# Sinkhorn-sorted attention and a bilinear FFN on one core: k and v of a head mixed together, v turned in two halves, units placed by a table

## The chip, the core and the metric

The kernel runs on one core of a Trainium2 chip. The core has TensorE (PE; its weight loads are shown as PEld), VectorE (DVE), ScalarE (ACT), GpSimd (POOL) and SyncE (SP), each with an instruction queue of its own that runs in order, and 16 engines for transfers (DMA). The metric is device time in microseconds (us) of one launch; less is better.

## What is computed

Cut to what matters (B, H, S, D = 4, 8, 768, 64; 8 blocks of 96 rows):

```python
P = sort_net                                   # 4, 8, 8, 8
for _ in range(5):
    P = np.exp(P - max(P, -1)); P = P / (sum(P, -1) + 1e-09)
    P = P / (sum(P, -2) + 1e-09)
k_sorted = einsum('bhij,bhjcd->bhicd', P, k_b)     # blocks of k mixed
v_sorted = einsum('bhij,bhjcd->bhicd', P, v_b)     # blocks of v mixed
attn = softmax(q_b @ k_sorted_b.T / sqrt(D))       # inside a block of 96
x = (attn @ v_sorted_b), heads side by side        # 3072 x 512
out = ((x @ w_a) * (x @ w_b)) @ w_out              # 512 -> 1536 -> 512
```

All inputs and the output are float32; the kernel works in bf16 with float32 sums in PSUM.

## The kernel before

Two heads form a pair `g`; four pairs make a batch, 16 pairs in all (`HP` = 4, `NPAIR` = 16). Row `6p + c` of a head lies on partition `p`, so each head's k, v and q arrive as a tile of 128 partitions by 6 chunks of 64 columns. `load_pair(g)` (line 93) issues the loads on GpSimd's queue, which convert float32 to bf16 on the way: k and v of both heads, and q for pairs from 4 on. Each tag has six buffers.

**Mixing.** `s_all` holds, for each head, P spread over the partitions. `pair_mix(g, "k")` (line 279) multiplies each chunk of k (64 weight columns) with `s_all` (128 moving columns): head 0 goes to PSUM partitions 0 to 63, head 1 to 64 to 127. That is 12 products for k and 12 for v. Four copies (ACT, ACT, then DVE, ACT) bring the results to `kT` and `vT`, of which there are three buffers (`NBUF`).

**Turning.** After this, k lies with its 64 columns on the partitions, as the scores need it. v has to be turned back: `turn_v(g)` (line 295) issues one transposing transfer of 128 x 1024 on SP's queue into `vs`. `pair_q(g)` (line 268) puts q of two heads side by side on GpSimd, and `turn_q(g)` (line 274) turns it on SP's queue.

**Scores and output.** `pair_scores(g)` (line 299) makes 2 x 8 score products and two exponentials on ACT (`eT`). `pair_o(g)` (line 314) calls `one_o` (line 244) twice: 8 products with a column of ones for the sum, reciprocal and scaling on DVE into `xp`. A transposing transfer on SP's queue then writes `xT`, which the FFN reads. `pair_o` also issues later loads, behind a `hold` (line 265): a copy of one element on GpSimd that waits until `xT` is there.

**The first batch** is done in two halves (blocks 0 to 3 and 4 to 7) by the functions named `half_` (lines 191 to 242); q is loaded for all of it at once (`q_first`), and q, v and x are turned by TensorE instead of by transfers.

**FFN.** `ffn_ab(b, m, t)` (line 349) makes 4 + 4 products of 384 columns (`pf`), a cast of `a` on ACT, and a product on DVE into `hT`. `ffn_out` (line 377) makes 12 products of 512 columns (`po`) in two steps, and a copy and a store.

**Order.** The order on the queues of all engines is the order in which the program issues instructions. `interleave(steps, units, spare, slow)` (line 451) runs the FFN steps of a batch and puts attention units of the next batch between them: M (mix), R (scores) and O (output), in the order of `units_full` (line 431), spread evenly by a formula. For batch 1 (24 steps) the units stand after steps 1, 2, 4, 5, 7, 8, 10, 11, 13, 14, 16, 17; for batches 2 and 3 (36 steps) after steps 1, 3, 5, 8, 10, 12, 15, 17, 19, 22, 24, 26. The order in both is M0, M1, R0, M2, R1, O0, M3, R2, O1, R3, O2, O3 (0 to 3 are the batch's pairs). M issues, in this order, k's mix, v's mix, `turn_v`, and for later pairs loads, `pair_q` and `turn_q` of the next pair.

Of the kernel before, what the change touches and what calls it, by code (L numbers as in the profile page):

```python
# [10 lines left out]
BF16 = mybir.dt.bfloat16  # L11
AF = mybir.ActivationFunctionType
# [10 lines left out]
def kernel(  # L23
# [43 lines left out]
    ld = ctx.enter_context(tc.tile_pool(name="ld", bufs=6))  # L67
# [18 lines left out]
    q_first = const.tile([P, H, W], BF16, name="q_first")  # L86
# [6 lines left out]
    def load_pair(g):  # L93
        base = 2 * g * S * D
        tiles = []
        for name, t in (("k2", k), ("v2", v), ("q2", q)):
            if g < HP and name == "q2":
                continue
            to = ld.tile([P, 2, W], BF16, tag=name, name=name)
            nc.gpsimd.dma_start(out=to, in_=_ap(t, base, [[W, P], [S * D, 2], [1, W]]))  # L100
            tiles.append(to)
        loaded[g] = tiles
# [5 lines left out]
    def load_ab(c):  # L108
        for w_ap, w_sb in ((moe_w_a, w_a_sb), (moe_w_b, w_b_sb)):
            nc.gpsimd.dma_start(  # L110
                out=w_sb[:, :, AB[c]:AB[c + 1]],
                in_=w_ap.rearrange("(kc p) n -> p kc n", p=P)[:, :, AB[c]:AB[c + 1]])
# [11 lines left out]
    for c in range(2):  # L124
        load_ab(c)
# [4 lines left out]
    kTs = [const.tile([P, S + PAD], BF16, name=f"kT{n}") for n in range(NBUF)]  # L130
    vTs = [const.tile([P, NB, P], BF16, name=f"vT{n}") for n in range(NBUF)]
    eTs = [const.tile([BLK, 2, 2, HB + PAD], BF16, name=f"eT{n}") for n in range(NBUF)]
    vss = [const.tile([P, NB, VW], BF16, name=f"vs{n}") for n in range(NBUF)]
    for t in kTs:
        nc.vector.memset(t[:, S:], 0.0)
        nc.vector.memset(t[:, HB:HB + PAD], 0.0)
    for t in vTs:
        nc.vector.memset(t[:, :, BLK:], 0.0)
# [6 lines left out]
    st = {}  # L145
# [29 lines left out]

    def first_q(hp):
        q_ps = psF.tile([P, NCH, P], BF16, tag="F", name="q_ps")
        for c in range(NCH):
            for e in range(2):
                nc.tensor.matmul(q_ps[e * D:(e + 1) * D, c, :],  # L180
                                 lhsT=q_first[:, 2 * hp + e, c * D:(c + 1) * D],
                                 rhs=ident, is_transpose=True)
        st["q_ps", hp] = q_ps

    def first_q_out(hp, eng):
        qT = const.tile([P, NB, NCH, CG], BF16, name=f"qT{hp}")
        copy(eng, qT.rearrange("p i c t -> p c i t"),
             st["q_ps", hp].rearrange("p c (i t) -> p c i t", i=NB))
        st["q", hp] = qT

    def half_mix(h, hp, what, eng, fill=0, cols=512):
        g = h * HP + hp
        src2 = loaded[hp][0 if what == "k" else 1]
        to = (kTs if what == "k" else vTs)[g % NBUF]
        mix = psF.tile([P, 512], FP32, tag="F", name="mixh")
        keep_busy(mix, fill, cols)
        for c in range(NCH):
            for e in range(2):
                nc.tensor.matmul(  # L199
                    _ap(mix, e * D * 512 + c * CG, [[512, D], [BLK, NBH], [1, CG]]),  # L200
                    lhsT=src2[:, e, c * D:(c + 1) * D],
                    rhs=s_all[:, 2 * hp + e, h * NBH:(h + 1) * NBH], start=True, stop=True)
        if what == "k":
            copy(eng, to[:, 0:HB], mix[:, 0:HB])
        else:
            copy(eng, to[:, 0:NBH, 0:BLK], _ap(mix, 0, [[512, P], [BLK, NBH], [1, BLK]]))

    def half_scores(h, hp):
        g = h * HP + hp
        kT, qT, eT = kTs[g % NBUF], st["q", hp], eTs[g % NBUF]  # L210
        sc = psA.tile([P, 2, 512], FP32, tag="A", name="sc")
        for i in range(NBH):
            for e in range(2):
                nc.tensor.matmul(  # L214
                    sc[:, e, i * BLK:(i + 1) * BLK],
                    lhsT=kT[e * D:(e + 1) * D, i * BLK:i * BLK + P],
                    rhs=qT[e * D:(e + 1) * D, h * NBH + i], start=True, stop=True)
        nc.scalar.activation(out=eT[:, 0, :, 0:HB], in_=sc[0:BLK, :, 0:HB],
                             func=AF.Exp, scale=float(scale))

    def half_v(h, hp):
        g = h * HP + hp
        vT, vs = vTs[g % NBUF], vss[g % NBUF]
        vs_ps = psF.tile([P, NBH, 2, D], BF16, tag="F", name="vs_ps")
        for i in range(NBH):
            nc.tensor.matmul(vs_ps[:, i], lhsT=vT[:, i], rhs=ident, is_transpose=True)  # L226
        nc.vector.tensor_copy(out=vs[0:BLK, 0:NBH, V0:V0 + P],
                              in_=vs_ps[0:BLK].rearrange("p i e d -> p i (e d)"))
# [39 lines left out]
    def pair_q(g):  # L268
        qc = qtp.tile([P, NCH, 2, D], BF16, tag="qc", name="qc", bufs=3)
        nc.gpsimd.tensor_copy(out=qc.rearrange("p c e d -> p e c d"),  # L270
                              in_=loaded[g][2].rearrange("p e (c d) -> p e c d", c=NCH))
        st[g, "qc"] = qc
# [6 lines left out]
    def pair_mix(g, what, engines):  # L279
        src2 = loaded[g][0 if what == "k" else 1]  # L280
        to = (kTs if what == "k" else vTs)[g % NBUF]
        pitch, whole = (BLK, S + PAD) if what == "k" else (P, NB * P)
        mix = psA.tile([P, 2, 512], FP32, tag="A", name="mix")
        for c in range(NCH):
            for e in range(2):
                nc.tensor.matmul(  # L286
                    mix[e * D:(e + 1) * D, c // 3, c % 3 * P:(c % 3 + 1) * P],
                    lhsT=src2[:, e, c * D:(c + 1) * D],
                    rhs=s_all[:, 2 * g + e], start=True, stop=True)
        for hf, eng in enumerate(engines):  # L290
            d1 = _ap(to, hf * 3 * CG, [[whole, P], [CG, 3], [pitch, NB], [1, CG]])
            s1 = _ap(mix, hf * 512, [[1024, P], [P, 3], [CG, NB], [1, CG]])
            copy(eng, d1, s1)

    def turn_v(g):
        nc.sync.dma_start_transpose(out=vss[g % NBUF][:, :, V0:V0 + P],
                                    in_=vTs[g % NBUF].rearrange("p i t -> p (i t)"))

    def pair_scores(g):
        kT, qT, eT = kTs[g % NBUF], st[g, "qT"], eTs[g % NBUF]  # L300
        for hf in range(2):
            sc = psA.tile([P, 2, 512], FP32, tag="A", name="sc")
            for i in range(NBH):
                for e in range(2):
# [3 lines left out]
                        lhsT=kT[e * D:(e + 1) * D, blk * BLK:blk * BLK + P],  # L308
# [5 lines left out]
    def pair_o(g):  # L314
        xp = att.tile([BLK, NB, 2, D], BF16, tag="xp", name="xp")
        for hf in range(2):
            one_o(eTs[g % NBUF], hf, vss[g % NBUF], hf * NBH, xp, NB)
        nc.sync.dma_start_transpose(
            out=xT_of(g // HP)[:, g % HP, :].rearrange("p (i t) -> p i t", i=NB),
            in_=xp.rearrange("p i e d -> p (i e d)"))  # L320
        if g == HP + 2:
            pair_q(2 * HP)
            turn_q(2 * HP)
        elif HP <= g < 2 * HP:
            hold(xT_of(1)[0:1, g % HP, 0:1])
            load_pair(2 * HP + (g - HP + 1) // 2)
        elif g >= 2 * HP and g + HP < NPAIR:
            load_pair(g + HP)
# [82 lines left out]
    def units_half():  # L411
        def M(hp):
            half_mix(1, hp, "k", "act")
            half_mix(1, hp, "v", "act")
# [16 lines left out]
    def units_full(b):  # L431
        def M(g):
            pair_mix(g, "k", ("act", "act"))
            pair_mix(g, "v", ("dve", "act"))
            turn_v(g)
            if g == 2 * HP:
                hold(kTs[g % NBUF][0:1, 0:1])
                load_pair(g + 3)
            if g in (HP + 1, HP + 3):
                spread(nc.gpsimd, p_col, (g - HP + 3) // 2 * 8, 8)  # L440
            if HP + 3 <= g + 1 < NPAIR and g + 1 != 2 * HP:
                pair_q(g + 1)
                turn_q(g + 1)

        g0 = b * HP
        order = [("M", 0), ("M", 1), ("R", 0), ("M", 2), ("R", 1), ("O", 0), ("M", 3),
                 ("R", 2), ("O", 1), ("R", 3), ("O", 2), ("O", 3)]
        what = {"M": M, "R": pair_scores, "O": pair_o}
        return [lambda w=w, n=n: what[w](g0 + n) for w, n in order]

    def interleave(steps, units, spare, slow=0):
        n, done = len(steps), 0
        for s, step in enumerate(steps):
            step()
            want = s + 1 if s < slow else -(-(s + 1) * len(units) // (n - spare))
            while done < min(want, len(units)):
                units[done]()
                done += 1

    with tc.manual_schedule(engines={ET.PE, ET.Pool, ET.SP, ET.Activation, ET.DVE}):  # L460
        if True:
# [69 lines left out]
            load_ab(2)  # L531
            load_ab(3)

            half_mix(0, 0, "k", "act", fill=2, cols=256)
            half_mix(0, 0, "v", "dve")
            to_columns(1)
            half_mix(0, 1, "k", "act")
# [4 lines left out]
            half_mix(0, 1, "v", "dve")  # L542
            half_mix(0, 2, "k", "act", fill=1)
# [3 lines left out]
            half_mix(0, 2, "v", "act")  # L547
            half_mix(0, 3, "k", "act", fill=1)
# [4 lines left out]
            half_mix(0, 3, "v", "act", fill=1)  # L553
# [14 lines left out]

        load_pair(4)
        spread(nc.gpsimd, p_col, 8, 8)  # L570
        load_pair(5)
        load_pair(6)
        pair_q(HP)
        turn_q(HP)
        load_pair(7)
        for c in range(3):
            load_out(c)
        for g in range(HP + 1, HP + 3):
            pair_q(g)
            turn_q(g)  # L580
# [4 lines left out]
        interleave(steps, units_half(), 1, 3)  # L585
# [3 lines left out]
        interleave(steps, units_full(1), 6)  # L589

        for b in range(1, B):
# [5 lines left out]
            interleave(steps, units_full(b + 1) if b + 1 < B else [], 8)  # L597
# [30 lines left out]
```

## Time and profile before

| | us |
|---|---|
| median of 3 runs | 245.27 |
| lowest, highest | 244.87, 245.83 |
| the profiled execution | 247.9 |
| its span, first to last instruction | 246.1 |

The clock granted to TensorE in the profiled execution is 1.000. The costliest groups and the last link of the chain of waits:

| group | instructions | busy us | mean ns |
|---|---|---|---|
| L341 pf, w_a and w_b, 384 columns | 760 | 155.3 | 327 |
| L382 po, 512 columns | 276 | 61.2 | 379 |
| L286 mix, k and v, 64 weight columns | 288 | 12.3 | 221 |
| L199 mixh, k and v, 64 weight columns | 192 | 6.0 | 198 |
| L249 o_ps | 256 | 11.4 | 193 |
| L276 qTf, transfer issued on SP | 12 | | lands after 6.3 us (median) |
| L296 vs, transfer issued on SP | 12 | | lands after 3.7 us (median) |
| L318 xT, transfer issued on SP | 12 | | lands after 4.2 us (median) |

How to read it: "busy" is the sum of what one instruction lasts, and products overlap, so the time that a row of products takes is read from the start of the first to the start of what follows. A line of the timeline gives start, length, engine, line, operation, output and inputs, and how many instructions of the kind stand there; in square brackets stands the idle time of the engine just before, and what ended it. A transposing transfer appears twice: as an issue on SP (SPq), whose length is the time that SP was held, and as a transfer (DMA) with its landing.

### The profile page before, as it was taken

The page shows a single profiled execution, that of the slowest core. Times are in us where ns is not written, and L with a number is a line of the kernel's source. Part 1 is how long each engine was busy: PE and PEld are TensorE (multiplying, and loading weights), DVE is VectorE, ACT ScalarE, POOL GpSimd, SP SyncE. Part 2 cuts the span into 40 slices and gives each one's busy share as a digit, 9 for nine tenths or more (in the row PEclk, how much of TensorE's full clock was granted, in tenths as well). Part 3 has the DMA queues.
Part 4 walks back from the last instruction along what each step waited for, and adds up shares of the span by engine and source line. Part 5 has one row for each costly group of instructions (what it writes and reads, how often), then busy time and mean ns, then how long its engine had stood idle before and what let it go on. Part 6 is the DMA issues. An engine that isn't in the chain of part 4 may idle for free.

```text
span 246.1 us, 5577 instructions
## 1 busy us (share of the span) xinstructions
PE 236.7 (96%) x2285; PEld 141.0 (57%) x2285; DVE 109.0 (44%) x255; ACT 103.8 (42%) x204; POOL 59.3 (24%) x82
## 2 busy tenths in 40 slices
PE   7899899996999999999999999999999999999994
PEld 7776666663654456666654465666654466665443
DVE  6665466542636144464652153363561244443110
ACT  3565764474551047546430056737420033333001
POOL 8678239410075072406611000000000000000000
PEclk9999999999999999999999999999999999999999
DMA  5999999999797999998997338312124210000132
GB/s 80 199 200 201 207 201 161 106 183 192 115 146 138 187 190 149 200 125 90 194 163 140 128 87 109 74 35 43 35 46 150 85 43 0 3 0 1 43 124 92
DMA packets 54474, 28.69 MB, mean 117 GB/s; under 512 B 33328, under 2 KB 51504, under 8 KB 54448
## 3 DMA queue, kind: packets, MB, share of 16 engines
q0 software_dynamic: 18832, 14.16, 42.6%
q1 hardware_dynamic: 35472, 14.11, 31.1%
q8 instruction: 18, 0.29, 0.5%
q10 hardware_dynamic: 144, 0.07, 0.1%
q14 instruction: 8, 0.07, 0.1%
HBM read 28.32 MB, written 6.29 MB: 141 GB/s over the span
## 4 chain that ended last, share of the span: by engine, by line
PE 88%; DMA 8%; DVE 2%; ACT 0%; issue 0%; POOL 0%
PE pf L341 48%; PE po L382 24%; DMA vs<-vT 5%; PE mix L286 4%; PE o_ps L249 3%; DMA q_first<-in_q_dram 3%; PE sc L306 2%; PE mixh L199 2%; PE po L402 1%; PE vs_ps L226 1%; PE xt_ps L240 1%; PE sc L214 1%; PE heat L171 1%; PE two L341 1%; DVE xp L255 1%; PE q_ps L180 0%
## 5 line engine op out<-in xcount | busy, mean ns | idle before, releaser
L362 DVE TENSOR_TENSOR hT<-a_sb,pf 128x384 bf16<-128x384 bf16 x95 | 52.6, 553 | 75.7 <-PE pf L341 44.3
L341 PE MATMUL pf<-xT,w_a_sb 128*128 128x384 bf16 x380 | 77.9, 327 | 0.0
L341 PE MATMUL pf<-xT,w_b_sb 128*128 128x384 bf16 x380 | 77.4, 326 | 0.0
L361 ACT CAST a_sb<-pf 128x384 bf16<-128x384 f32 x95 | 45.5, 479 | 60.9 <-PE pf L341 39.6
L382 PE MATMUL po<-w_out_sb,hT 128*128 128x512 bf16 x276 | 61.2, 379 | 0.0
L341 PEld LDWEIGHTS <-w_b_sb 128*128 128x128 bf16 x384 | 37.5, 98 | 25.2 <-issue 0.6
L341 PEld LDWEIGHTS <-w_a_sb 128*128 128x128 bf16 x384 | 34.7, 98 | 22.2
L382 PEld LDWEIGHTS <-hT 128*128 128x128 bf16 x276 | 26.3, 97 | 30.7
L165 ACT COPY o_sb<-po 128x512 f32<-128x512 f32 x12 | 7.0, 586 | 50.7 <-PE po L382 46.1
L167 DVE COPY o_sb<-po 128x512 f32<-128x512 f32 x11 | 7.6, 692 | 39.7 <-PE po L382 30.7
L311 ACT ACTIVATE eT<-sc 96x768 bf16<-96x768 f32 x24 | 18.1, 802 | 4.3 <-PE sc L306 4.3
L255 DVE TENSOR_TENSOR xp<-o_ps,rec 96x512 bf16<-96x512 f32 x24 | 16.5, 687 | 0.8
L270 POOL COPY qc<-q 128x768 bf16<-128x768 bf16 x12 | 9.9, 836 | 28.0 <-DMA q<-in_q_dram 15.3
L249 PE MATMUL o_ps<-vs,eT 96*128 96x65 bf16 x256 | 11.4, 193 | 2.7 <-DMA vs<-vT 2.3
L249 PEld LDWEIGHTS <-eT 96*128 96x128 bf16 x256 | 10.3, 97 | 5.8 <-DMA vs<-vT 2.7
L165 ACT CAST kT<-mix 128x384 bf16<-128x384 f32 x24 | 10.3, 482 | 6.7 <-PE mix L286 6.7
L100 POOL DMA_DIRECT2D v<-in_v_dram x16 | 11.7, 728 | 5.6 <-DMA w_a_sb<-in_moe_w_a_dram 2.2
L100 POOL DMA_DIRECT2D k<-in_k_dram x16 | 11.8, 737 | 3.5 <-PE pf L341 2.8
L171 PE MATMUL heat<-warm 128*128 128x128 bf16 x98 | 8.4, 259 | 1.3 <-DVE warm L84 1.3
L100 POOL DMA_DIRECT2D q<-in_q_dram x12 | 8.8, 731 | 2.0 <-DMA w_b_sb<-in_moe_w_b_dram 1.2
L171 PEld LDWEIGHTS <-warm 128*128 128x128 bf16 x103 | 8.0, 119 | 1.7 <-DVE warm L84 1.3
L253 DVE RECIPROCAL rec<-o_ps 96x8 f32<-96x8 f32 x32 | 6.3, 197 | 5.5 <-PE o_ps L249 5.5
(78 smaller groups left out, 144.2 us busy)
## 6 DMA issues: line engine op xcount, KB each, us to landing
out_dram<-o_sb SPq DMA_DIRECT2D x17, 256.0 KB, 2.0
k<-in_k_dram POOLq DMA_DIRECT2D x16, 192.0 KB, 7.1
v<-in_v_dram POOLq DMA_DIRECT2D x16, 192.0 KB, 7.5
q<-in_q_dram POOLq DMA_DIRECT2D x12, 192.0 KB, 8.5
w_out_sb<-in_moe_w_out_dram POOLq DMA_DIRECT2D x3, 512.0 KB, 16.4
out_dram<-o_sb SPq DMA_DIRECT2D x12, 128.0 KB, 2.5
w_a_sb<-in_moe_w_a_dram POOLq DMA_DIRECT2D x2, 512.0 KB, 13.5
w_b_sb<-in_moe_w_b_dram POOLq DMA_DIRECT2D x2, 512.0 KB, 14.7
```

The costliest lines, as they stand in the source:

```text
L100: nc.gpsimd.dma_start(out=to, in_=_ap(t, base, [[W, P], [S * D, 2], [1, W]]))
L165: nc.scalar.copy(out=out, in_=in_)
L171: nc.tensor.matmul(ps[:, 0:cols], lhsT=warm[:, 0:P], rhs=warm[:, 0:cols], start=True, stop=True)
L249: nc.tensor.matmul(o_ps[:, e, i * (D + 1):(i + 1) * (D + 1)], lhsT=eT[:, hf, e, i * BLK:i * BLK + P], rhs=vs[0:BLK, i0 + i, V0 - 1 + e * ( ...
L255: nc.vector.tensor_tensor(out=_ap(xp, i0 * 2 * D, [[nxp * 2 * D, BLK], [D, 2], [2 * D, NBH], [1, D]]), in0=_ap(o_ps, 1, [[1024, BLK], [511 ...
L270: nc.gpsimd.tensor_copy(out=qc.rearrange("p c e d -> p e c d"), in_=loaded[g][2].rearrange("p e (c d) -> p e c d", c=NCH))
L286: nc.tensor.matmul(mix[e * D:(e + 1) * D, c // 3, c % 3 * P:(c % 3 + 1) * P], lhsT=src2[:, e, c * D:(c + 1) * D], rhs=s_all[:, 2 * g + e], ...
L311: nc.scalar.activation(out=eT[:, hf, :, 0:HB], in_=sc[0:BLK, :, 0:HB], func=AF.Exp, scale=float(scale))
L341: nc.tensor.matmul(pf[:, 0:HW], lhsT=w_sb[:, kc, m * P:(m + 1) * P], rhs=x_cols(b, kc, t), start=(kc == 0), stop=(kc == KA - 1))
L361: nc.scalar.copy(out=a_sb, in_=pf[:, 0:HW])
L362: nc.vector.tensor_mul(out=hT[:, m, t * HW:(t + 1) * HW], in0=a_sb, in1=ab[1][:, 0:HW])
L382: nc.tensor.matmul(v["po"], lhsT=hTs[b][:, m, c * P:(c + 1) * P], rhs=w_out_sb[:, m, :], start=(m == 0), stop=(m == KO - 1))
```

## The change

- `load_pair` puts k of head 0, v of both heads and k of head 1 in one tile (`kv`, four slots). There are four such buffers, and four of q.
- A new `regroup(g)` on GpSimd copies `kv` as 32-bit elements so that a chunk's four groups of 64 columns lie together (`kvc`, five buffers). k and v of head 0 are then 128 adjacent columns, and v and k of head 1 too. `pair_q` also copies as 32-bit elements.
- `pair_mix(g, e, engines)` mixes k and v of head `e` by six products of 128 weight columns. The result has k on partitions 64e to 64e + 63 and v on the other 64, in `kvs[n][e]`. The second half of the first batch does the same in `half_mix` with `h` = 1; the first half keeps products of 64 weight columns.
- `turn_v` issues two transposing transfers of 64 partitions, one for each head. For pair 7 it moves from the mix to between the output of pair 4 and its transfer to `xT`. `half_v` with `h` = 1 turns v by eight ordinary products with columns of the identity and float32 results, instead of four transposing ones.
- `interleave` takes the places of the units from a table, and in batch 1's units M3 and O0 are exchanged.
- The loads of the last quarter of w_a and w_b come after the regroups of pairs 0 and 1; the regroups of pairs 2 and 3 stand before the load of pair 4. Some `hold`s and loads of later pairs move by a unit. `qT` of the first batch shares a tile with `q_first`.

```diff
-    ld = ctx.enter_context(tc.tile_pool(name="ld", bufs=6))
+    ld = ctx.enter_context(tc.tile_pool(name="ld", bufs=4))
+    kvp = ctx.enter_context(tc.tile_pool(name="kvp", bufs=5))
...
+        kv = ld.tile([P, 4, W], BF16, tag="kv", name="kv")
+        for t, to in ((k, _ap(kv, 0, [[4 * W, P], [3 * W, 2], [1, W]])), (v, kv[:, 1:3])):
             nc.gpsimd.dma_start(out=to, in_=_ap(t, base, [[W, P], [S * D, 2], [1, W]]))
...
+    def regroup(g):
+        to = kvp.tile([P, NCH, 4, D], BF16, tag="kvc", name="kvc")
+        nc.gpsimd.tensor_copy(
+            out=to.bitcast(U32).rearrange("p c n d -> p n c d"),
+            in_=loaded[g][0].bitcast(U32).rearrange("p n (c d) -> p n c d", c=NCH))
+        st["kvc", g] = to
...
-    kTs = [const.tile([P, S + PAD], BF16, name=f"kT{n}") for n in range(NBUF)]
-    vTs = [const.tile([P, NB, P], BF16, name=f"vT{n}") for n in range(NBUF)]
+    kvs = [[const.tile([P, NB, P], BF16, name=f"kv{n}{e}") for e in range(2)]
+           for n in range(NBUF)]
...
+    def kv_of(g, e, c):
+        return st["kvc", g][:, c, 2 * e:2 * e + 2].rearrange("p s d -> p (s d)")
+
+    def k_rows(e):
+        return slice(e * D, (e + 1) * D)
+
+    def v_rows(e):
+        return slice((1 - e) * D, (2 - e) * D)
...
         for c in range(NCH):
-            for e in range(2):
+            if h == 1:
+                nc.tensor.matmul(_ap(mix, c * CG, [[512, P], [BLK, NBH], [1, CG]]),
+                                 lhsT=kv_of(hp, e, c), rhs=s_all[:, 2 * hp + e, NBH:],
+                                 start=True, stop=True)
+                continue
+            for n in range(2):
...
         for i in range(NBH):
-            nc.tensor.matmul(vs_ps[:, i], lhsT=vT[:, i], rhs=ident, is_transpose=True)
+            if h == 0:
+                nc.tensor.matmul(vs_ps[:, i], lhsT=kv[1][:, i], rhs=ident, is_transpose=True)
+                continue
+            for e in range(2):
+                nc.tensor.matmul(vs_ps[:, i, e], lhsT=kv[e][:, i], rhs=ident[:, v_rows(e)],
+                                 start=True, stop=True)
...
-    def pair_mix(g, what, engines):
+    def pair_mix(g, e, engines):
         mix = psA.tile([P, 2, 512], FP32, tag="A", name="mix")
         for c in range(NCH):
-            for e in range(2):
-                nc.tensor.matmul(
-                    mix[e * D:(e + 1) * D, c // 3, c % 3 * P:(c % 3 + 1) * P],
-                    lhsT=src2[:, e, c * D:(c + 1) * D],
-                    rhs=s_all[:, 2 * g + e], start=True, stop=True)
+            nc.tensor.matmul(mix[:, c // 3, c % 3 * P:(c % 3 + 1) * P], lhsT=kv_of(g, e, c),
+                             rhs=s_all[:, 2 * g + e], start=True, stop=True)
...
     def turn_v(g):
-        nc.sync.dma_start_transpose(out=vss[g % NBUF][:, :, V0:V0 + P],
-                                    in_=vTs[g % NBUF].rearrange("p i t -> p (i t)"))
+        for e in range(2):
+            nc.sync.dma_start_transpose(
+                out=vss[g % NBUF][:, :, V0 + e * D:V0 + (e + 1) * D],
+                in_=kvs[g % NBUF][e][v_rows(e)].rearrange("p i t -> p (i t)"))
...
+        if g == HP:
+            turn_v(2 * HP - 1)
         nc.sync.dma_start_transpose(
             out=xT_of(g // HP)[:, g % HP, :].rearrange("p (i t) -> p i t", i=NB),
             in_=xp.rearrange("p i e d -> p (i e d)"))
         if g == HP + 2:
             pair_q(2 * HP)
             turn_q(2 * HP)
+            regroup(2 * HP)
...
-            pair_mix(g, "k", ("act", "act"))
-            pair_mix(g, "v", ("dve", "act"))
-            turn_v(g)
-            if g == 2 * HP:
-                hold(kTs[g % NBUF][0:1, 0:1])
-                load_pair(g + 3)
+            pair_mix(g, 0, ("act", "act"))
+            pair_mix(g, 1, ("dve", "act"))
+            if g != 2 * HP - 1:
+                turn_v(g)
+            if g == 2 * HP + 1:
+                hold(kvs[g % NBUF][0][0:1, 0, 0:1])
+                load_pair(g + 2)
...
+            if HP + 2 <= g + 1 < NPAIR and g + 1 != 2 * HP:
+                regroup(g + 1)
...
+        if b == 1:
+            order[5:7] = order[6:4:-1]
...
+        regroup(0)
+        regroup(1)
+        for n in range(2):
+            load_ab(3, n)
+        regroup(2)
+        regroup(3)
         load_pair(4)
         spread(nc.gpsimd, p_col, 8, 8)
         load_pair(5)
         load_pair(6)
+        regroup(4)
         pair_q(HP)
         turn_q(HP)
         load_pair(7)
+        regroup(5)
         for c in range(3):
             load_out(c)
...
-        interleave(steps, units_half(), 1, 3)
+        interleave(steps, units_half(), (1, 2, 3, 4, 4, 4, 5, 5, 6, 7, 7, 8, 9, 9, 10, 11))
...
-        interleave(steps, units_full(1), 6)
+        interleave(steps, units_full(1), (1, 2, 4, 5, 7, 9, 10, 12, 13, 15, 16, 17))
...
-            interleave(steps, units_full(b + 1) if b + 1 < B else [], 8)
+            interleave(steps, units_full(b + 1) if b + 1 < B else [],
+                       (1, 4, 8, 10, 13, 15, 17, 20, 21, 24, 25, 28))
```

## The prediction

> **What bounds the kernel now.** I read the page first (busy shares), then the busy time by stretches of the span, the order in time on TensorE around a mix block, the chain of waits around 49 to 62 us, and the order in time on SP's and GpSimd's queues.
>
> ```profile
> PE 236.7 (96%) x2285; PEld 141.0 (57%) x2285; DVE 109.0 (44%) x255; ACT 103.8 (42%) x204; POOL 59.3 (24%) x82
> ...
> 45.00:62.00 17.00, 14.69 (x185) 8.98 (x184) 6.66 (x13) 10.35 (x21) 1.40 (x2) 1.00 1.35 171
> 62.00:87.00 25.00, 24.55 (x213) 12.76 (x210) 10.55 (x23) 7.71 (x14) 8.03 (x12) 1.00 0.94 148
> 87.00:142.00 55.00, 55.00 (x493) 31.71 (x492) 24.16 (x48) 23.79 (x47) 18.55 (x26) 1.00 1.01 150
> 142.00:196.00 54.00, 54.00 (x486) 31.07 (x485) 23.68 (x47) 23.80 (x47) 0.00 (x0) 1.00 0.34 76
> ```
>
> The columns of the last four are the stretch and its length, busy time of PE, PEld, DVE, ACT and POOL with instructions, the granted clock, the transfer engines' share and GB/s. TensorE bounds it: from 87 to 196 us it is never idle, at full clock, so there the time is TensorE's issue time and nothing else. One stretch has a real hole: 45 to 62 us lacks 2.31 us. So two questions decide: what TensorE's work shrinks by, and what becomes of the stretch before 87 us, where transfers set the pace.
>
> **TensorE's part.** The mix of k and of v was two products of 64 weight columns each (heads 0 and 1), now one of 128 per head: 24 instructions become 12. The naive reading halves the block. The order in time says otherwise:
>
> ```profile
> 98.42 0.81 PE L341 MATMUL pf<-xT,w_a_sb 128*128 128x384 bf16 x4
> 99.08 0.81 PE L341 MATMUL pf<-xT,w_b_sb 128*128 128x384 bf16 x4
> 99.82 0.53 PE L286 MATMUL mix<-s_all,k 128*64 128x128 bf16 x12
> 100.18 0.50 PE L286 MATMUL mix<-s_all,v 128*64 128x128 bf16 x12
> 100.61 0.66 PE L341 MATMUL pf<-xT,w_a_sb 128*128 128x384 bf16 x3
> ```
>
> From first to next start the block takes 100.61 - 99.82 = 0.79 us for 24, 33 ns each, though each lasts 219 ns: two narrow products run side by side, a pair in some 66 ns. What does a full one cost? The warm-up has 12 with fresh 128x128 weights and 128 moving columns:
>
> ```profile
> 10.24 0.84 PE L171 MATMUL heat<-warm 128*128 128x128 bf16 x12
> ```
>
> 0.84 less one latency of 0.22 over 11 steps: 56 ns. Hence 12 x 56 = 0.67 us. The rest is switching: four 384-column products take 0.65 (4 x 0.1625; 98.42 to 99.08 with rounding), but from 99.08 to 99.82 passed 0.74, so entering the narrow shape costs 0.09; leaving is in the 0.79. The block costs 0.79 + 0.09 = 0.88 and will cost 0.67: 0.21 x 12 pairs = 2.5 us. If the gaps belonged to something other than the shape, the saving would be 0.
>
> The second half of batch 0 (half_mix with h = 1, four times) goes the same way:
>
> ```profile
> 33.31 0.81 PE L341 MATMUL pf<-xT,w_b_sb 128*128 128x384 bf16 x4
> 34.06 0.38 PE L199 MATMUL mixh<-s_all,k 128*64 128x64 bf16 x12
> 34.27 0.36 PE L199 MATMUL mixh<-s_all,v 128*64 128x64 bf16 x12
> 34.56 0.82 PE L341 MATMUL pf<-xT,w_a_sb 128*128 128x384 bf16 x4
> ```
>
> 0.50 + 0.10 = 0.60 before. After, 12 with 64 moving columns; nearest row is o_ps (65 columns, 16 in 0.67, less 0.19, over 15: 32 ns): 0.38. Saved 0.21 x 4 = 0.84. half_v with h = 1 turns v by 8 products of 64 columns (8 x 32 = 0.26) where 4 of 128 stood (4 x 56 = 0.22): +0.03 x 4 = 0.13 back. Its copy now reads f32 (as o_sb's 692 ns for 512 columns against 416): up to 0.28 on DVE, hidden by DVE's idleness there and 1.3 us of ffn before half_o needs it; without cover, 1.1 us. Six buffers are zeroed at the start where three vT (0.42 us in the chain) and three kT (0.14) were: 0.3 more on DVE, before the first q lands at 9.4; hidden. Scores, the copies' number and the last 50 us stay. The first half (h = 0) keeps its products. Sum on TensorE: 2.5 + 0.84 - 0.13 = 3.2 us less; of that 8 x 0.21 = 1.7 lies in the two full stretches.
>
> **GpSimd's part.** Each pair gets a regroup (128 x 768 four-byte elements; 16 in all). Nearest row:
>
> ```profile
> L270 POOL COPY qc<-q 128x768 bf16<-128x768 bf16 x12 | 9.9, 836 | 28.0 <-DMA q<-in_q_dram 15.3 <-issue 12.7
> ```
>
> By elements 0.84 us, by bytes 1.67; pair_q, now 384 elements, 0.42 to 0.84. I take 1.2 and 0.6. Regroups 0 and 1 stand ahead of the last w_a, w_b loads, 2 and 3 ahead of pair 4's. Those queue with bytes ahead of them: the loads run at some 200 GB/s from the first slices to the eighth, w_a's median landing is 13.5 us after issue, so 2.4 to 5 us of lateness in issue leave the stream full. Cover gone: a dry stream, from about 2.5 us a regroup. Regroups 4 and 5 wait for their loads and hold back w_out's issue by some 1 us, with loads of pairs 6 and 7 still queued. Pair 4's loads now share four buffers, not six, and wait for pair 0's first-half mix and regroup, both done by then. Cost 0, up to 2. Later, regroup(9) is the tightest: behind the hold for xT of pair 7, three issues of 0.73 and pair_q(9) it ends some 4 us after batch 1 begins; its mix, moved by the table from the third step to the fourth, comes 5.9 us after (4 x 1.3 + 0.67). Cost 0, up to 1.
>
> **The crossbars of 64 rows.** turn_v issues two transposes for one, on SP's ordered queue; 12 more issues. No 64-row transpose is in the trace. Bounds: two halves cost what one whole does (0 more), or each a whole (1.23 us of SP more per pair and its transfer again). Less than one whole is excluded for the issue, one instruction more. Bytes are the same, so I take the transfer as unchanged and the issue as 1.2 more. In batches 2 and 3 there lie over 10 us between mix and its use: hidden. In batch 1's pairs it is not, because of this:
>
> ```profile
> 44.15 5.07 SPq L276 DMA_TRANSPOSE qTf<-qc  x1
> 49.27 7.55 SPq L296 DMA_TRANSPOSE vs<-vT  x1
> ...
> 49.27 12.14 DMA vs<-vT
> 61.41 0.04 issue
> ...
> 61.45 0.67 PE L249 MATMUL o_ps<-vs,eT 96*128 96x65 bf16 x16 [2.31 <-DMA vs<-vT]
> ```
>
> While weight loads fill the engines a transpose needs 12.1 us to land and even its issue sticks for 7.55.
>
> The Trainium skill ("DMA: Bandwidth & Descriptors", Rules for kernel authors) speaks against this part: two transfers to disjoint partition halves serialize, one over 128 partitions is better. By that rule the two would at best equal one; nothing in this trace tests it, and the sum above already has no gain from the split.
>
> **The table's part.** In batch 1's units the mix of pair 7 now precedes the output of pair 4, which goes from after step 8 to after step 10. Before, it could start at 61.45 - 2.31 = 59.1. After: 59.1 - 0.71 (half stage) - 3 x 0.21 + 2 x 1.30 + 0.67 = 61.0. The transfer before was there at 61.4; one q transpose (pair 6) that stood ahead of it now stands behind, worth about 0.8 at the pace after the loads, so v of pair 4 lands at about 60.8 (59 to 64). But the moved mix overwrites the buffers this transpose reads: its copies (0.48 each on ACT) now wait for the landing, behind them on ACT the casts of a, and the two PSUM buffers of the output. Output start: 60.8 + 2 x 0.48 = 61.8, a stall of 0.8. At that start the kernel has done two steps and a mix more than at 61.45 before: 0.71 + 4 x 0.21 + 2.31 - 0.8 = 3.1 us ahead.
>
> What is late next: SP must then issue q of 6, v of 6 (2), q of 7, v of 7 (2, moved behind pair 4's output), then xT of pair 4: at 1.23 each, from about 59.5, xT(4) issues near 66.9 (63.7 before), and GpSimd's hold on it delays pair 8's loads from 68.1 to about 71.3. Their q is needed for qTf(8), behind which SP queues xT(7), which batch 1 reads:
>
> ```profile
> 78.21 0.86 POOL L270 COPY qc<-q 128x768 bf16<-128x768 bf16 x1
> ...
> 81.26 2.79 SPq L318 DMA_TRANSPOSE xT<-xp  x1
> ...
> 86.27 0.18 POOL L266 COPY held<-xT 1x1 bf16<-1x1 bf16 x1 [7.20 <-DMA xT<-xp]
> ```
>
> xT(7) landed by 86.2, batch 1 began at 87.1: 0.9 of slack, 1.4 to its use. Loads took 6.4 us (68.1 to about 74.5), so q(8) is there at 77.7, xT(7) issues at 80 to 81, lands at 84 to 85; batch 1 wants it at 87.1 - 3.1 + 0.5 = 84.5. Stall 0 to 2, taken 0.7. Last, in batches 2 and 3 an output follows its scores by one step instead of two: exponentials of 2 x 0.80 against a step of 1.30, some 0.1 x 4; taken 0.3.
>
> **Sum** against the profiled execution (span 246.1; 247.9 in all; the median of the runs is 245.27): 3.1 - 0.7 + 1.7 - 0.3 = 3.8 less. The difference is carried to the median: 245.27 - 3.8 = 241.5; I say 241.4.
>
> **Rivals.** (1) Transfers keep up: no new stall, all 3.2 and the 2.31 come through: 5.5 less, 239.8. For it: the loads' bytes are unchanged; against: the 0.9 us slack of xT(7). (2) The gain before 87 us is eaten, batch 1 begins where it did, and only 1.7 remains, or the switching gaps stay though the shapes go: 243.6 to 244.9. For it: xT(7)'s gate depends on transfers, not TensorE. Against the second: o_ps (full columns) follows pf at its plain pace. (3) Slower: SP's queue in batch 1's pairs. If a half costs 2.5 us instead of 1.2 (issues of 3.4 to 7.55 stand there), the five halves of pairs 5 to 7 before xT(4) add 6.5 us to its chain; batch 1 begins 3.4 late rather than 2.4 early, 1.7 comes back: 247.0. It decides from about 2.2 us a half. Against it: after the loads end at 59 us all issues fall to 1.23. (4) GpSimd slower than 2.5 us a regroup: the stream runs dry, some 249.
>
> **How the numbers follow.** Forecast 0.42, (1) 0.25, (2) 0.20, (3) 0.10, (4) 0.03. What a measurement tells from no change is 0.5%, 1.2 us: faster means below 244.0. The first two and half of (2) are faster: 0.77; same 0.12; slower 0.11. Range 239.0 to 245.3: from a little below (1) through (2); the forecast's own is 240 to 243.
>
> **What would show it.** Mix blocks of 0.67 without the 0.09 before them; regroups of 0.84 to 1.67 on GpSimd; the stall at pair 4's output under 2.31 and named by v's transfer or ACT's copies; a short hole where batch 1 begins, named xT; none from there to the end. Wrong would make it: mix blocks over 0.8, halves of v that land one after the other as wholes, or a new hole at scores of pair 6 (q behind four halves).

## The result, and the profile after

| | before | changed |
|---|---|---|
| median, us (4 runs each) | 245.39 | 242.01 |
| lowest, highest | 244.87, 245.83 | 241.73, 242.83 |
| span of the profiled execution | 246.1 | 240.2 |

The ratio of the changed kernel's time to that before is 0.9869, with a 95% interval of 0.9838 to 0.9900: 3.4 us less. The two spans differ by more, 5.9 us; why is told below. The page of the changed kernel, its busy shares and its two groups on GpSimd:

```profile
PE 232.2 (97%) x2100; PEld 141.3 (59%) x2109; DVE 110.0 (46%) x252; ACT 104.0 (43%) x204; POOL 67.6 (28%) x98
...
L111 POOL COPY kvc<-kv 128x768 uint32<-128x768 uint32 x16 | 13.2, 834 | 0.1
L299 POOL COPY qc<-q 128x384 uint32<-128x384 uint32 x12 | 6.2, 518 | 19.8 <-DMA q<-in_q_dram 13.0 <-issue 6.6
```

A regroup of 768 four-byte elements costs 834 ns where 768 two-byte ones had cost 836: the time went by the elements, not by the bytes. TensorE's order in time around a mix of the changed kernel (start, length, what):

```profile
97.41 0.81 PE L371 MATMUL pf<-xT,w_b_sb 128*128 128x384 bf16 x4
98.06 0.83 PE L312 MATMUL mix<-s_all,kvc 128*128 128x128 bf16 x12
98.73 0.81 PE L371 MATMUL pf<-xT,w_a_sb 128*128 128x384 bf16 x4
```

Four products of 384 columns take their 0.65 us up to the mix, and the mix 0.67: the two gaps are gone. What a block is worth shows over the whole of the batch that both kernels run without a hole. In the chain of waits (start, length, what) it lies between the first `pf` after one batch's output and the next such; before:

```profile
141.66 1.30 PE pf L341 x8
142.96 0.79 PE mix L286 x24
...
196.18 0.97 PE pf L341 x6
```

and in the changed kernel:

```profile
136.94 1.30 PE pf L371 x8
138.24 0.67 PE mix L312 x12
...
190.56 0.49 PE pf L371 x3
```

54.52 us became 53.62: 0.90 for four mix blocks, 0.23 each.

The hole at pair 4's output is gone; its products start at 60.38 with two more FFN steps and a mix done. A new one opens where batch 1 begins. TensorE's order, and the chain of waits that leads there, in the changed kernel:

```profile
82.19 0.65 PE L371 MATMUL pf<-xT,w_a_sb 128*128 128x384 bf16 x3
83.66 0.32 PE L371 MATMUL pf<-xT,w_a_sb 128*128 128x384 bf16 x1 [0.82 <-DMA xT<-xp]
```

```profile
67.55 7.38 DMA xT<-xp
...
75.52 0.86 POOL kv L100 x2
...
76.94 0.73 POOL q L104
77.67 0.52 POOL qc L299
...
79.52 4.09 DMA xT<-xp
83.66 0.97 PE pf L371 x5
```

It is to be read from below: the first batch-1 step has xT of three pairs and waits for the fourth, pair 7's. That transfer went out at 79.52, behind pair 8's q on SP. GpSimd copied this q at 77.67, after it had issued pair 9's loads, and those stood behind a hold on xT of pair 5, which took 7.38 us to land: pair 8's loads had begun at 66.7, just before.

### The profile page after: what moved, and what is told of

It reads as the page before. It is cut to its first block, busy times and chain, and to the rows that moved or that the text cites. A ratio compares the mean times of both kernels' runs of the same rounds, so it can differ in the third digit from the quotient of the medians.

```text
span 240.2 us, 5255 instructions
## 1 busy us (share of the span) xinstructions
PE 232.2 (97%) x2100; PEld 141.3 (59%) x2109; DVE 110.0 (46%) x252; ACT 104.0 (43%) x204; POOL 67.6 (28%) x98
## 3 DMA queue, kind: packets, MB, share of 16 engines
q1 hardware_dynamic: 35856, 14.11, 30.9%
## 4 chain that ended last, share of the span: by engine, by line
PE 85%; DMA 5%; DVE 4%; POOL 1%; ACT 1%; issue 1%; SPq 0%; POOLq 0%
PE pf L371 52%; PE po L412 19%; DMA xT<-xp 5%; PE mix L312 3%; PE o_ps L278 3%; PE sc L333 2%; PE po L432 1%; PE mixh L224 1%; PE xt_ps L269 1%; PE sc L237 1%; DMA p_nat<-in_sort_net_dram 1%; DVE xp L284 1%; PE vs_ps L254 1%; ACT p_nat L521 1%; PE two L371 1%
## 5 line engine op out<-in xcount | busy, mean ns | idle before, releaser
L412 PE MATMUL po<-w_out_sb,hT 128*128 128x512 bf16 x267 | 60.8, 379 | 0.5
L371 PEld LDWEIGHTS <-w_a_sb 128*128 128x128 bf16 x384 | 35.4, 98 | 21.2
L175 ACT CAST kv<-mix 128x384 bf16<-128x384 f32 x36 | 16.1, 481 | 6.0 <-PE mix L312 5.0
L111 POOL COPY kvc<-kv 128x768 uint32<-128x768 uint32 x16 | 13.2, 834 | 0.1
L100 POOL DMA_DIRECT2D kv<-in_k_dram x16 | 11.7, 730 | 3.0 <-PE pf L371 2.1
L100 POOL DMA_DIRECT2D kv<-in_v_dram x16 | 11.7, 728 | 2.1 <-DMA w_b_sb<-in_moe_w_b_dram 1.5
L299 POOL COPY qc<-q 128x384 uint32<-128x384 uint32 x12 | 6.2, 518 | 19.8 <-DMA q<-in_q_dram 13.0
L312 PE MATMUL mix<-s_all,kvc 128*128 128x128 bf16 x144 | 10.0, 219 | 0.0
L312 PEld LDWEIGHTS <-kvc 128*128 128x128 bf16 x144 | 9.1, 98 | 1.5
```

The source lines that it names most:

```text
L111: nc.gpsimd.tensor_copy(out=to.bitcast(U32).rearrange("p c n d -> p n c d"), in_=loaded[g][0].bitcast(U32).rearrange("p n (c d) -> p n c d ...
L175: nc.scalar.copy(out=out, in_=in_)
L312: nc.tensor.matmul(mix[:, c // 3, c % 3 * P:(c % 3 + 1) * P], lhsT=kv_of(g, e, c), rhs=s_all[:, 2 * g + e], start=True, stop=True)
L371: nc.tensor.matmul(pf[:, 0:HW], lhsT=w_sb[:, kc, m * P:(m + 1) * P], rhs=x_cols(b, kc, t), start=(kc == 0), stop=(kc == KA - 1))
L412: nc.tensor.matmul(v["po"], lhsT=hTs[b][:, m, c * P:(c + 1) * P], rhs=w_out_sb[:, m, :], start=(m == 0), stop=(m == KO - 1))
```

## The experiments

Times are medians beside the kernel before on the same chip; a ratio is to that kernel. "Changed" is the changed kernel.

**1. The kernel before, profiled again.** No edit.

> The kernel before, unchanged, profiled once more. Its profiled execution had a span of 246.1 us, while its median of 245.3 us means a span of some 243.5. Theory A (the hole at pair 4's output is a chance of that execution, set by when the weight loads end): span 243 to 244, the hole under 1 us and the weight loads over before 59 us. Theory B (the hole is in every execution): span 243 to 246 with a hole of 2 us or more again, and something else is shorter.

Span 245.7, one time of 247.48. Neither theory held as stated: A wanted a span of 243 to 244 and a hole under 1 us, B a hole of 2 us or more, and the hole at pair 4's output was 1.22. TensorE's order at two of its holes:

```profile
9.85 0.86 PE L180 MATMUL q_ps<-ident,q_first 128*64 128x128 bf16 x24 [1.32 <-DMA q_first<-in_q_dram]
...
61.00 0.67 PE L249 MATMUL o_ps<-vs,eT 96*128 96x65 bf16 x16 [1.22 <-DMA vs<-vT]
```

Like the first profiled execution (0.96 and 2.31) it waited long for the second half of q and at pair 4's output. Runs 3 and 4, with the same loads, did not wait for the second half of q, had their first `pf`, the FFN's first product, at 20.7 (21.4 and 22.1 in these two) and spans of 243.8 and 243.9; the median of before, less the 1.8 us that lie around a span, is 243.6. So both profiles of before were late ones. That the hole of 2.31 was larger than a common execution has is worked out from this: run 3, which differs from before in the halves alone, shows 0.55 + 0.27, but no profile of before itself lies near its median.

**2. Narrow products again in the changed kernel.**

```diff
-            nc.tensor.matmul(mix[:, c // 3, ...], lhsT=kv_of(g, e, c),
-                             rhs=s_all[:, 2 * g + e], start=True, stop=True)
+            for s in range(2):
+                nc.tensor.matmul(mix[s * D:(s + 1) * D, c // 3, ...],
+                                 lhsT=st["kvc", g][:, c, 2 * e + s],
+                                 rhs=s_all[:, 2 * g + e], start=True, stop=True)
```

> The changed kernel with the full pairs' mixes done again by two products of 64 weight columns each (24 instead of 12), from the regrouped tile; the rest stays. Theory (switching between narrow and full shapes costs 0.21 us a block, 12 blocks): 2.5 us slower than the changed kernel, so about 244.5 us, mix blocks back at 0.88 us. Rival (the gaps have nothing to do with the shape): within 0.3 us of the changed kernel, about 242 us, and blocks of about 0.67 us plus the same gaps.

245.24 us, ratio 0.9985 (0.9964 to 1.0006): no longer distinct from before, and above the changed kernel by 2.8 us (its ratio of 0.9869) to 3.2 us (its ratio of 0.9856 in run 9, on the same chip). TensorE's order there:

```profile
154.24 0.81 PE L373 MATMUL pf<-xT,w_b_sb 128*128 128x384 bf16 x4
154.99 0.86 PE L313 MATMUL mix<-s_all,kvc 128*64 128x128 bf16 x24
155.78 0.82 PE L373 MATMUL pf<-xT,w_a_sb 128*128 128x384 bf16 x4
```

Both gaps are back (0.75 for four products of 0.65, then 0.79 for the block), with the same data, layout and copies. The second gap is seen when the last two of the 24 are taken alone:

```profile
155.62 0.22 PE L313 MATMUL mix<-s_all,kvc 128*64 128x128 bf16 x2
```

From 154.99 to 155.62 are 11 pairs: 0.08 us for the first and 0.056 for each other, which is also the pace of the full products (12 in 0.67). From the last pair to the next `pf` it is 0.16 instead of 0.056. So twice as many instructions cost nothing by their number; the time lies at the two changes of shape, 0.09 us going in and 0.10 coming out, and 0.02 at the first pair.

**3. Two halves of v, alone**, in the kernel before.

```diff
-        nc.sync.dma_start_transpose(out=vss[g % NBUF][:, :, V0:V0 + P],
-                                    in_=vTs[g % NBUF].rearrange("p i t -> p (i t)"))
+        for e in range(2):
+            nc.sync.dma_start_transpose(
+                out=vss[g % NBUF][:, :, V0 + e * D:V0 + (e + 1) * D],
+                in_=vTs[g % NBUF][e * D:(e + 1) * D].rearrange("p i t -> p (i t)"))
```

> The kernel before with v turned by two transposes of 64 rows instead of one of 128, nothing else. Theory (halves cost 1.2 us of SP each but the transfer costs the same bytes; only batch 1's pairs can feel it): 0 to 1 us slower than before, 245.4 to 246.4 us; each half's issue about 1.2 us where nothing contends, transfers of the same number of 256-byte packets. Rival (each half costs a whole transfer): 2 us or more slower and twice the small packets for v.

245.51 us, ratio 0.9992 (0.9975 to 1.0009): no change that shows, at most 0.2 us slower by the interval. The transfers' queue and issues of this run:

```profile
q1 hardware_dynamic: 35856, 14.11, 31.8%
...
vs<-vT SPq DMA_TRANSPOSE x24, 3.6
```

SP's queue has 384 packets more than before (35472) at the same 14.11 MB, 32 for each added issue; had each half been a whole, 12 x 1024 packets of 256 bytes would have come. An issue of a half held SP for 1.26 us (median). A half lands after 3.6 us, a whole had after 3.7.

**4. The table alone**, in the kernel before: the places, the exchange of M3 and O0 in batch 1, and pair 7's v turned behind pair 4's output, as in the diff above.

> The kernel before with the changed kernel's table of places, the exchanged M3 and O0 in batch 1 and pair 7's turn of v moved behind pair 4's output, nothing else. Theory (the exchange hides what hole there is at pair 4's output, but xT of pair 7 comes late by a like amount): 0 to 1.5 us faster than before, 243.9 to 245.4 us. Rival (the table is the main gain): 2.5 us or more faster, under 243 us. Other rival (without the cheaper mixes it only moves waits): slower than 245.9 us.

245.18 us, ratio 0.9982 (0.9963 to 1.0002): no change that is clear of noise. No hole at pair 4's output any more, but, in TensorE's order:

```profile
83.49 0.65 PE L343 MATMUL pf<-xT,w_a_sb 128*128 128x384 bf16 x3
85.28 0.32 PE L343 MATMUL pf<-xT,w_a_sb 128*128 128x384 bf16 x1 [1.14 <-DMA xT<-xp]
```

The table takes one wait away and makes the other.

**5 and 11. xT of pair 7 ahead of pair 8's q**, in the changed kernel, twice.

```diff
-        if g == HP + 2:
+        if g == 2 * HP - 1:
             pair_q(2 * HP)
             turn_q(2 * HP)
             regroup(2 * HP)
-        elif HP <= g < 2 * HP:
+        if HP <= g < 2 * HP and g != HP + 2:
```

> The changed kernel with pair 8's q copy, q transpose and regroup moved from pair 6's output to pair 7's, so that SP issues xT of pair 7 ahead of pair 8's q. Theory (the hole of 0.82 us where batch 1 begins is xT of pair 7 behind pair 8's q, which waits behind GpSimd's hold and loads): the hole goes and 0.6 to 0.9 us with it, 241.2 us; xT of pair 7 issues at about 75 instead of 79.5 us. Rival (xT is late because its transfer meets pair 9's loads): the hole stays within 0.3 us, 242 us.

> xT of pair 7 ahead of pair 8's q, once more, on the same chip. Theory (it takes the hole away whenever it would come): 0.5 to 1.0 us faster than the changed kernel beside it, about equal to the doubled regroup. Rival (the earlier gain was chance): within 0.4 us of it.

In both profiles the hole is gone; TensorE's order in the first of them:

```profile
82.23 0.81 PE L371 MATMUL pf<-xT,w_a_sb 128*128 128x384 bf16 x4
82.88 0.81 PE L371 MATMUL pf<-xT,w_b_sb 128*128 128x384 bf16 x4
```

SP's order, and GpSimd's wait for this xT, there:

```profile
74.54 1.21 SPq L347 DMA_TRANSPOSE xT<-xp  x1
77.59 1.22 SPq L306 DMA_TRANSPOSE qTf<-qc  x1
...
79.57 0.18 POOL L295 COPY held<-xT 1x1 bf16<-1x1 bf16 x1 [1.25 <-DMA xT<-xp]
```

SP now issues xT of pair 7 at 74.5 us, in the second profile at 75.8, instead of 79.5, and it lands at 79.5 and 81.5, over 2 us before batch 1 needs it. Runs 8 and 12 have the same order, and no hole there either. The times are 241.81 and 241.29, ratios 0.9826 (0.9798 to 0.9855) and 0.9848 (0.9821 to 0.9875). The changed kernel had 0.9869, and 0.9856 (0.9830 to 0.9882) beside the second. That SP's order makes the hole is shown, by these issues and landings more than by the missing hole, which run 7 lacks too; a gain in time is not, the intervals overlap.

**6. The old table in the changed kernel**: old places, M3 and O0 as before, pair 7's v turned in its mix.

> The changed kernel with the old places and the old order of M3 and O0 in batch 1, and pair 7's v turned with its mix again; wide products, regroup and halves stay. Theory (wide products carry the change, the table adds about what it did alone, some 0.4 us): 242.0 to 243.0 us, with a hole of 0.5 to 2 us at pair 4's output. Rival (the regroup needs the table: mixes of pairs 9 and 12 wait for GpSimd): holes of over 0.5 us before mixes in batches 1 and 2, 243.5 us or more.

241.38 us, ratio 0.9825 (0.9799 to 0.9851), against a changed kernel of 0.9869 and 0.9856. Its only new hole, in TensorE's order:

```profile
57.66 0.84 PE L278 MATMUL o_ps<-vs,eT 96*128 96x65 bf16 x16 [0.32 <-DMA vs<-kv]
```

None stands before a mix, and batch 1 begins without one. The theory had 242.0 to 243.0 us and a hole of 0.5 to 2: it gave the table too much. Once the mixes are wide the table brings nothing that shows.

**7 and 10. Every regroup twice**, in the changed kernel: the copy in `regroup` stands there a second time.

> The changed kernel with every regroup copied twice to the same place (16 copies of 0.83 us more on GpSimd). Theory (the regroup is hidden; spare time before pair 9's mix is some 1.4 us): within 0.5 us of the changed kernel, 241.5 to 242.5 us. Rival (GpSimd's queue is near the path through loads and holds): 1 us or more slower, 243 us and up.

> Every regroup copied twice, once more, on the same chip as the changed kernel. Theory (it was 1 us faster because pair 8's loads start 0.9 us later and meet xT of pair 5 less, which takes away the hole where batch 1 begins): 0.5 to 1.2 us faster than the changed kernel beside it, no hole there. Rival (chance, or another chip): within 0.4 us of it.

241.04 us, ratio 0.9800 (0.9777 to 0.9822), then 241.38, 0.9830 (0.9806 to 0.9854), beside 242.10 of the changed kernel. 13 us more on GpSimd cost nothing: the regroup is hidden, and its rival falls. It came out faster, and my reason for that fell with the second run, whose profile had the hole at its largest:

```profile
84.56 0.32 PE L374 MATMUL pf<-xT,w_a_sb 128*128 128x384 bf16 x1 [1.71 <-DMA xT<-xp]
```

Why it should be faster, or whether it is, stays open.

**8 and 12. Copies of batch 0's output moved**, on top of run 5: in 8 even columns go to DVE and odd ones to ACT, in 12 only column 1 goes from DVE to ACT.

```diff
-            copy("act" if c % 2 == 0 else "dve", o_sb, v["po"])
+            copy("act" if (c % 2 == 0) == (b > 0) else "dve", o_sb, v["po"])         # 8
+            copy("act" if c % 2 == 0 or (b, c) == (0, 1) else "dve", o_sb, v["po"])  # 12
```

> As the run with xT of pair 7 first, and in batch 0 the output copies of even columns go to DVE and of odd ones to ACT (the other way before), so that DVE no longer has a copy ahead of pair 6's scaling. Theory (the hole of 0.41 us at pair 7's output is DVE's lateness by that copy of 0.69 us): 0.3 to 0.4 us faster than that run, about 240.9 us. Rival (the next wait takes its place): same as that run within 0.2 us.

> As the run with xT of pair 7 first, with one copy moved: batch 0's output columns 1 go from PSUM by ACT instead of DVE; the copies of columns 3 and 5, which wait for stores, stay on DVE. Theory (of the two effects of the exchanged copies the good one is the copy ahead of pair 6's scaling, the bad one the copy that waits for a store ahead of ACT's casts): the hole of 0.41 us at pair 7's output falls to about 0.1 and no hole of over 0.5 us comes after it; 0.3 us faster than the run before, the fastest of all. Rival: ACT's exponentials of pair 7 come late by the copy, hole as before, same time.

243.22 and 242.58 us, ratios 0.9888 and 0.9887. The hole of 0.41 at pair 7's output fell to 0.07 and 0.06, as thought. But a larger one came 14 us later. Run 12, order in time on DVE and TensorE:

```profile
86.85 0.69 DVE L177 COPY o_sb<-po 128x512 f32<-128x512 f32 x1 [9.32 <-DMA out_dram<-o_sb]
87.46 0.54 DVE L392 TENSOR_TENSOR hT<-a_sb,pf 128x384 bf16<-128x384 bf16 x1
87.60 0.81 PE L371 MATMUL pf<-xT,w_b_sb 128*128 128x384 bf16 x4 [3.04 <-DVE o_sb L177]
```

The last copy of the batch waits for a store to free one of three buffers, and behind it on DVE stands the FFN's product. In run 8 the same copy waited 9.0 us on ACT, and TensorE 2.48. So the engine does not matter, and my second guess of run 12 (safe on DVE) was wrong. In the changed kernel the same copy waits for the store too (DVE idle for 6.4 us) and starts at 84.34, and TensorE does not wait for it. That is not because the hole at xT covers it: in runs 5 and 11, which have no such hole, the copy starts at 84.0 and 84.9, and TensorE does not wait either. What differs in 8 and 12 is the store that frees the buffer: issued at 80.4 and 80.6, it took 6.0 and 6.1 us to land, against 4.4 and 4.5 in runs 5 and 11. Pair 10's loads went out beside it, at 79.3 and 79.5 instead of 80.0 and 82.0; whether they made it slow is not shown. A fourth buffer was not tried.

**9. The changed kernel again.** No edit.

> The changed kernel, unchanged, beside the next three on one chip. Theory (its hole where batch 1 begins is a matter of some 1 us in when xT of pair 5 lands, and comes and goes): 241.5 to 242.5 us; in this profile the hole is between 0 and 1.2 us.

242.10 us, ratio 0.9856 (0.9830 to 0.9882). The four products where batch 1 begins took 0.87 us instead of 0.65: this time the hole was 0.2. Over executions of the same or nearly the same program it was 0.82, 0.2, 1.71 (run 10) and 0 (run 7). The theory, that the landing of pair 5's xT sets it, does not carry run 10: there that xT landed at 74.5, as here (74.6), and SP issued pair 7's xT at 79.1 in both, but this took 5.5 us to land instead of 4.0. Why is open.

## Why the prediction held, point by point

| term | predicted, us | measured |
|---|---|---|
| a mix block | 0.88 to 0.67, 0.21 saved | 0.23 saved |
| 12 blocks | 2.5 | 2.7; run 2 gives 2.8 to 3.2 |
| second half of batch 0 | 0.71 saved | 0.4 saved |
| regroup, q copy | 1.2, 0.6, hidden | 0.83, 0.52, hidden (run 7) |
| two halves for a whole | issue 1.2 more, bytes the same, 0 | 1.22 (median) an issue, bytes the same, 32 small packets more an issue, 0 (run 3) |
| hole at pair 4's output | 2.31 removed, 0.8 left | removed, 0 left; but 2.31 was no common value |
| where batch 1 begins | 0.7 lost, named xT | 0.82 and 0.2 lost in two profiles, named xT |
| output one step after scores | 0.3 lost | none seen |

**Right: what the wide products save and why.** Not the number of instructions, which the side-by-side pace made worthless, but the entry and exit of the narrow shape. Run 2 brings gaps and time back with nothing else changed. One detail was off: a pair inside a block takes 56 ns, not 66; the prediction had spread the exit over the block.

**Right: the place of the new hole; wrong: the reason.** The prediction had xT of pair 4 issued near 66.9 us and pair 8's loads near 71.3, so that pair 8's q came late. Measured, they went out at 63.7 and 66.7, and this q had landed by 75.4. It was copied late, at 77.67, because GpSimd, in order, had first to pass the hold on xT of pair 5 and issue pair 9's loads. That this xT took 7.38 us because it met pair 8's loads is argued from its time alone: in the kernel before it was issued at 72.1, four us after these loads, and landed after 3.3. Run 5 shows that SP's order then carries the lateness to xT of pair 7. So the size, 0.7 for 0.82, agreed by luck. (In run 2's profile GpSimd did wait 1.22 us for pair 8's q itself.)

**Wrong in size: the second half of batch 0.** The prediction let all of TensorE's saving through. There two holes grew: 0.10 to 0.23 and 0.61 to 0.86. The second of them, in the kernel before:

```profile
26.88 0.32 PE L341 MATMUL two<-xT,w_a_sb 128*128 128x384 bf16 x1 [0.61 <-DVE hT L362]
```

The order in time of the changed kernel:

```profile
24.93 0.49 ACT L391 CAST a_sb<-pf 128x384 bf16<-128x384 f32 x1
...
25.44 0.55 DVE L392 TENSOR_TENSOR hT<-a_sb,two 128x384 bf16<-128x384 bf16 x1 [0.73 <-ACT a_sb L391]
...
26.05 0.32 PE L371 MATMUL two<-xT,w_a_sb 128*128 128x384 bf16 x1 [0.86 <-DVE hT L392]
```

For these two blocks ACT and DVE bound the path: TensorE is done sooner and waits longer, and 0.38 of the 0.71 us is lost. This is read from the profiles; no run changes this stage alone.

**Wrong in size: the hole at pair 4's output.** The sum took 2.31 us from one execution and had v of pair 4 land at about 60.8 (59 to 64). It landed at 56.9, before its output was due, so neither hole nor remainder came; the last weight load had landed at 56.4 us instead of 60.3. Part of this is more than chance: with the same first `pf` (20.6 to 21.0) that load landed at 58.0 and 58.1 with the old loads (runs 3 and 4), and at 55.8 to 57.4 in eight profiles with the new ones. The sum had set the effect of the moved loads at 0, and no run takes it apart. Run 6 agrees with it: with the old table only 0.32 of the hole is left. Chance entered in two ways: before's profile was some 2.5 us later than its median, which the sum carried over unweighed, and the changed kernel's was not. Against the profiled span the sum was short (3.8 for 5.9); against the median it was near (3.8 for 3.4). Worked out from common sizes, as an estimate, it is: 2.7 for the blocks, 0.4 for the half stage, 0.8 for the hole as in run 3, 0.4 for the table's smaller waits between pair 4's mix and batch 1 (38.5 us before without its hole, 38.1 in run 4), less some 0.8 at batch 1's begin: 3.5. So the forecast of 241.4 came near 242.01 in part by luck: the hole was counted 0.7 too high and the half stage 0.3, while the blocks were counted 0.2 too low, the table's smaller waits (0.4) not at all, and a loss of 0.3 at the outputs did not come.

**Two readings that were wrong.** The loads do not run at some 200 GB/s up to the eighth slice: the page before has 161 in the seventh and 106 in the eighth. And issues do not all fall to 1.23 us after the loads end: the prediction's own line has 2.79 at 81.26. Neither term that rests on them (0 for the moved loads, 0 for the halves) cost anything that shows.

**The rivals.** The dearer halves (3) and a GpSimd that starves the loads (4) fell with runs 3 and 7. (2), the gain eaten before batch 1, fell too: batch 1's first product starts at 82.19 us, at 86.98 in the profile before and at 84.88 in run 3, and the switching gaps went with the narrow shapes. (1), no new stall, is what the profiles of runs 5 and 7 show, but they took 241.12 and 241.02 us and not 239.8: the 2.31 was not there to be gained.

**The Trainium skill's rule** ("DMA: Bandwidth & Descriptors", Rules for kernel authors) that a transfer cut into partition halves gains nothing agrees with run 3: 0.9992, neither gain nor loss. Whether the halves go one after the other, as the page has it, run 3 does not tell. The halves were needed for the layout, and the issue more that each pair costs does not show in the time.

## What to carry to other kernels

Here two narrow products side by side cost as much as one wide one (56 ns); what they cost beyond that was each change between narrow and full shapes (some 0.1 us), so count the changes of shape, not the instructions. Before a hole in a profile enters a sum, ask whether a common execution has it: compare the profiled time with the median, and profile twice. A wait that does no harm (here a copy behind a store, up to 84.9 us) becomes the bound when it ends some 2 us later (86.5 and 86.9 in runs 8 and 12), whichever engine it stands on. And where a forecast agrees in size, check its links too: here the hole came where it was foretold, for another reason.

## What the runs showed of the hardware beyond what was expected

- GpSimd copied 768 four-byte elements per partition in 834 ns and 768 two-byte ones in 836; 384 four-byte ones took 518. Viewing pairs of bf16 as one 32-bit element saved 0.32 us of a 0.84 us copy.
- A transpose of 64 partitions held SP for 1.22 us (median), one of 128 for 1.23: the issue does not shrink with the rows, the packets do.
- The first loads end up to 1.5 us apart over these profiles (first `pf` at 20.6 to 22.1 us), and the last weight load landed anywhere between 55.8 and 60.3 us.
